# Second layer of a top-1 mixture: 128 tokens in one form and 448 in the other, with a new order of work

## The chip, the cores and the metric

The kernel runs on one core of a Trainium2 chip. The metric is the device time of one execution in microseconds, lower is better. The engines are named as in the profile: PE is TensorE, with PEld for its weight loads, DVE is VectorE, ACT is ScalarE, POOL is GpSimd, and SP is SyncE, which issues all DMAs here.

## The reference, cut to what matters

An attention over 32 memory slots feeds a mixture of 8 experts, of which each token uses one. The expert of a token is the argmax of its own gate or, where a local gate is 0.5 or more, that of the token before it.

```python
# q, k, v: (8, 8, 576, 64); phi: (8, 8, 576, 32); w1: (8, 512, 1024); w2: (8, 1024, 512)
a = softmax(phi, axis=2)                     # over the 576 tokens
k_m = einsum('bhsm,bhsd->bhmd', a, k); v_m = einsum('bhsm,bhsd->bhmd', a, v)
x = softmax(q @ k_m.T / 8) @ v_m             # heads side by side: (8, 576, 512)
for b in range(8):
    for s in range(576):
        e = fresh argmax of x[b, s] @ w_gate, or the expert of token s - 1
        p = softmax(x[b, s] @ w_gate)
        out[b, s] = p[e] * (relu(x[b, s] @ w1[e]) @ w2[e])
```

## The kernel before, in words

The kernel works batch by batch, 576 tokens each. For each batch it takes the expert of the first token and runs all 576 tokens through that expert; the probability of a token is set to zero where it has another expert. Pairs of batch and expert that remain are listed on the chip, and a loop at the end adds them.

For one batch, `hidden` computes the first layer: the matrix `G` (value memory times w1, from `w_pg` and `w_G`) against the attention weights `ah` and `al`. Values are held as two parts, high and low, in fp32r, and each product takes three matmuls: high by high, and both mixed terms. The result goes through the ReLU on ACT (L1109) and its low part through DVE (L1111) into `h`. Tokens are taken in `HALVES`, 256 and 320, so that `hidden` makes 4 groups of 12 matmuls of 256 columns and 8 groups of 6 of 320 columns.

The second layer has two forms. In the token form (`second`, L1139 to L1141) a block of 128 tokens stands as weights in the array and W2 streams past with 512 columns; the block takes 8 x 3 matmuls. In the turned form (`second_turned`, L1189 to L1191) a block of 128 output columns of W2 stands as weights and tokens stream past; there are 4 such blocks with 8 x 3 matmuls each, and each ends with a transpose on DVE (L1195) and a multiply by the probabilities on POOL (L1196). Batches 0 to 6 do tokens 0 to 255 in the token form (two blocks) and 256 to 575 in the turned form (320 columns). Batch 7 does everything in the token form: four blocks of 128, of which the last is done in two halves of 256 columns, and one block of 64 tokens, whose high and low parts stand side by side as 128 weights (L1163).

W2 is split by `w_split` on ACT and POOL, one of 8 pieces at a time; `t_evict` and `t_store` bring out a block of the token form, `o_store` the turned part with four DMAs.

The order of all work is written out by hand. `SCHEDULE` is a text with one line for each `yield` of `hidden`, `second` and `second_turned`; the steps of a line are issued to the engines' queues right after that group of matmuls. Steps are named with their batch, as `2 choice` or `2 pg 0`, and look ahead: most of the attention of batch b + 1 is issued among the matmuls of batch b. Each engine works through its queue in order. `BANKS` says for the small matmul steps which of the three PSUM pools their tile is taken from: "a" (3 banks), "h" (3 banks, first layer) or "o" (2 banks, `po` of the second layer).

Steps that are named below: `pg 0` and `pg 1` multiply the value memory by w1 (L1068, needs w1 loaded); `choice` finds the first token's expert on DVE (L871 to L873); `expert` lets SP read it, upon which SP issues `w1 0` (L1034); `a psc` makes scores on PE, `a turn` transposes them (L786); `g cols` makes columns of probabilities (L1001 on DVE, L1007 to L1017 on ACT); `g present` is a reduction on DVE (L992, L993); `z qT 0` is a transpose on DVE (L741); `warm b` and `warm u` are matmuls on zeros.

Of the kernel before, what the change touches and what calls it, by code (L numbers as in the profile page):

```python
# [48 lines left out]
0 split 1, 1 z qT 0, 0 split 2
0 split 3, 1 pT  # L50
1 q 1
1 a qT 0, 0 g kept

0 g carry, 0 split 4, 1 a qT 1


0 split 5, 0 split 6, 1 z qT 1, 0 at store
2 phi, 0 g exp, 1 kvT, 1 a psc, 0 split 7, 1 pgg
1 a turn
0 g prob  # L60
1 a mx, 0 g cols, 1 a sub, 2 colmax
1 a exp, 2 q 0, 0 evict 0, 1 a sum, 1 a inv, 1 a mul
# [18 lines left out]
2 kvT
2 a psc

1 split 1, 2 a turn
1 split 2
1 split 3
1 split 4, 2 z psc, 2 z turn, 2 a mx, 3 q 0, 2 pgg
3 colmax, 2 ggt, 1 split 5, 2 z mx
1 split 6, 2 a sub, 0 store 0, 0 store
1 split 7, 2 z sub, 0 store 1  # L90
2 a exp, 3 z qT 0
3 pm, 3 mc

2 a sum
3 kv, 2 z exp, 2 z sum, 2 z inv, 2 a inv, 1 g cols

3 pm2, 2 a mul, 1 evict 0, 2 z mul, 1 g present, 3 cx
2 a at

1 evict 1, 2 z at, 3 sub 1, 3 a qT 0, 2 g pl, 2 pl0, 2 g lt, 2 a ah, 3 exp 1, 2 g L  # L100
3 sub 0, 2 choice, 2 g fresh, 2 g kept, 3 q 1, 3 z qT 1
# [15 lines left out]
2 split 4, 3 a sub  # L120
# [8 lines left out]
4 kv, 3 z sub, 3 expert, 3 w1 0, 4 asum, 3 z exp, 3 z sum
2 g cols, 3 z inv  # L130
3 z mul
3 z at, 2 g present, 4 a qT 0, 1 kv store, 4 q 1, 4 pkv 0, 3 w1 1, 4 pkv 1, 5 phi, 3 w2 0, 3 pg 0, 5 q 0, 4 sums, 3 g pl, 3 z ah
3 g lt, 2 evict 0, 4 rinv, 4 z qT 0, 3 g L

3 G 0, 4 kvn, 4 z qT 1, 3 z al, 4 a qT 1, 4 pT
4 kvT, 4 a psc, 2 evict 1, 3 g fresh, 4 a turn, 4 a mx, 3 pg 1, 4 pgg, 5 colmax, 4 a sub, 4 ggt, 3 g kept
3 a al, 2 kv store


4 a exp, 4 a sum, 3 at store, 3 G 1  # L140
# [3 lines left out]
4 a inv, 3 g carry, 3 w2 1, 5 a qT 0  # L144


5 pm, 4 a mul, 4 a at
5 mc, 3 split 0

4 pl0, 4 z psc, 4 z turn, 4 choice, 5 pm2, 5 kv, 5 cx, 5 sub 0  # L150
4 expert, 3 split 1
5 sub 1, 4 z mx, 3 split 2, 4 a ah, 4 kv store, 4 a al, 3 split 3

5 q 1

3 g exp
3 split 4, 3 split 5, 5 exp 0, 2 store 1, 4 z sub  # L160


4 w1 0, 4 w1 1, 5 exp 1

3 split 6, 5 asum, 4 pg 0, 4 z exp, 3 g prob, 4 z sum, 5 a qT 1, 4 z inv, 5 pkv 0, 6 phi, 3 split 7, 5 z qT 0, 3 g cols, 5 pkv 1, 5 sums, 3 g present, 4 z mul, 5 z qT 1
# [3 lines left out]
5 rinv, 5 kvn, 4 z at, 4 g pl, 4 pg 1  # L169
6 colmax, 6 pm, 3 evict 0, 5 pT, 4 g lt, 4 G 1, 4 g L, 4 w2 0, 6 mc, 4 z ah, 5 kvT  # L170
3 store 0, 4 g fresh


4 z al, 4 G 0
5 pgg, 5 a psc, 5 a turn, 5 z psc, 2 store, 5 a mx, 5 ggt, 6 pm2, 6 cx, 5 kv store, 5 z turn

5 a sub, 6 sub 1, 6 q 0, 6 exp 1, 5 z mx, 4 g kept
3 evict 1, 6 sub 0
# [5 lines left out]
4 split 0, 4 split 1, 4 split 2, 5 a exp, 5 z sub, 5 a sum, 5 a inv, 4 split 3, 4 w2 1, 4 split 4, 4 split 5  # L184

6 exp 0, 5 a mul, 6 kv, 4 at store

5 a at, 6 q 1
5 z exp
2 store 0, 4 split 6, 5 z sum  # L190

5 a ah, 5 z inv, 4 g exp, 5 pl0, 5 choice


5 z mul, 5 expert
5 z at
6 asum, 5 w1 0, 5 w1 1

6 a qT 0, 7 phi, 6 pkv 0, 5 pg 0, 6 pkv 1, 6 sums, 4 split 7, 6 z qT 0, 4 g carry, 5 G 0
# [8 lines left out]
6 a exp, 6 a sum, 5 g exp, 7 mc, 5 split 0, 4 g present  # L210
# [48 lines left out]

5 g present
6 split 7
6 g exp, 6 g kept
7 pl0, 7 z psc


5 store, 7 choice
7 z turn, 7 z mx, 7 kv store, 7 z sub, 7 a ah  # L270
7 z exp, 7 expert, 6 g carry, 7 z sum

7 w1 0

7 w1 1

7 z inv, 7 z mul
7 z at
7 z ah, 7 pg 0, 5 store 1, 7 pg 1, 7 a al, 6 g prob, 7 g pl, 6 g cols, 6 evict 0
6 evict 1  # L280

7 G 0, 7 g lt
7 g L, 7 w2 0, 7 g fresh, 7 at store
6 g present
# [1261 lines left out]
```

## Time and profile before

| | us |
|---|---|
| median of three runs (397.38 to 398.92) | 398.43 |
| the profiled execution | 401.71 |
| its span, first to last instruction | 399.9 |
| PE busy in it | 386.5 |
| DVE busy in it | 282.4 |

The span leaves out 1.8 us that lie around it. Busy time is a sum over the span; it does not say which engine a stage waits for. Matmuls overlap each other, so that the mean of one is a latency and not its cost.

### The profile page before, as it was taken

The numbers are of one execution on the slowest core, as the hardware profiler recorded it, in microseconds if no ns is written. First come the engines' busy times: TensorE is split into PE (matmuls) and PEld (weight loads), VectorE is DVE, ScalarE is ACT, GpSimd is POOL, SyncE is SP. The second block draws the span as 40 slices with busy tenths as digits, with TensorE's granted clock in tenths as the row PEclk, the third lists the DMA queues.
The fourth block names the chain that finished last, engine by engine and source line by source line (L and its number), as shares of the span: only waits on it lengthen the run. The fifth ranks groups of instructions, "written<-read, shape, count | busy, mean of one in ns | idle before, by whom it ended". The sixth has DMA issues, their size and how long they took to land.

```text
span 399.9 us, 10792 instructions
## 1 busy us (share of the span) xinstructions
PE 386.5 (97%) x4336; PEld 335.2 (84%) x4336; DVE 282.4 (71%) x702; ACT 176.7 (44%) x437; POOL 151.1 (38%) x162
## 2 busy tenths in 40 slices
PE   8689999999998999999999999999999999999996
PEld 4476988899887887889878998799888998799885
DVE  4477899988988589786797779757845678456330
ACT  2236644447352584326653552515633653435311
POOL 1006471525330963129504741309412651057000
PEclk9789999999999999999999999999999999999999
DMA  7959869988969787979787937998680028702011
GB/s 226 315 188 330 169 166 263 354 218 190 294 165 373 171 303 174 297 221 301 243 256 178 324 82 277 351 233 225 216 290 8 2 80 318 268 1 67 27 41 57
DMA packets 115918, 82.59 MB, mean 207 GB/s; under 512 B 70100, under 2 KB 89560, under 8 KB 115864
## 3 DMA queue, kind: packets, MB, share of 16 engines
q1 hardware_dynamic: 115864, 81.86, 69.4%
q8 instruction: 35, 0.57, 0.6%
q14 instruction: 19, 0.16, 0.1%
HBM read 66.60 MB, written 15.24 MB: 205 GB/s over the span
## 4 chain that ended last, share of the span: by engine, by line
PE 48%; SPq 5%; DMA 5%; DVE 3%; issue 1%; ACT 1%; DVEq 0%
PE ph L1101 15%; PE po L1139 5%; PE po L1140 5%; PE po L1141 5%; DMA att_d<-at 4%; SPq L493 4%; PE po L1189 4%; PE po L1191 4%; PE po L1190 4%; PE pg L1068 2%; PE pkv L648 2%; DMA q_t<-in_q_dram 1%; PE po L1163 1%; PE psc L773 1%; DVE qT L741 1%
## 5 line engine op out<-in xcount | busy, mean ns | idle before, releaser
L1056 POOL TENSOR_TENSOR w2l<-raw,w2h 128x512 fp32r<-128x512 f32 x64 | 83.3, 1326 | 58.7 <-ACT w2h L1055 35.2
L1101 PE MATMUL ph<-ah,Gh 128*128 128x256 f32 (+1 forms) x256 | 73.4, 301 | 0.5 <-DVE h L1111 0.4
L1101 PE MATMUL ph<-ah,Gl 128*128 128x256 f32 (+1 forms) x256 | 72.0, 295 | 0.0
L1189 PE MATMUL po<-h,w2l 128*128 128x320 f32 x224 | 71.1, 317 | 0.1
L1111 DVE SCALAR_TENSOR_TENSOR h<-ph,h 128x320 fp32r<-128x320 f32 (+2 forms) x104 | 52.3, 517 | 24.8 <-ACT h L1109 24.4
L1191 PE MATMUL po<-h,w2h 128*128 128x320 f32 x224 | 69.2, 309 | 0.0
L1190 PE MATMUL po<-h,w2h 128*128 128x320 f32 x224 | 69.2, 309 | 0.0
L1109 ACT ACTIVATE h<-ph 128x320 fp32r<-128x320 f32 (+1 forms) x96 | 46.8, 492 | 38.6 <-PE ph L1101 38.3
L1139 PE MATMUL po<-w2h,h 128*128 128x512 f32 (+1 forms) x152 | 58.9, 388 | 0.0
L1140 PE MATMUL po<-w2l,h 128*128 128x512 f32 (+1 forms) x152 | 57.6, 379 | 0.0
L1141 PE MATMUL po<-w2h,h 128*128 128x512 f32 (+1 forms) x152 | 57.5, 378 | 0.0
L1101 PE MATMUL ph<-al,Gh 128*128 128x256 f32 (+1 forms) x256 | 55.0, 296 | 0.0
L842 POOL TENSOR_TENSOR al<-at,ah 128x576 fp32r<-128x576 f32 (+1 forms) x18 | 23.1, 1288 | 73.7 <-ACT ah L838 73.7
L1101 PEld LDWEIGHTS ph<-ah,Gh 128*128 128x128 f32 x256 | 48.1, 188 | 2.6 <-DVE h L1111 0.9
L1196 POOL TENSOR_TENSOR oT<-oT,gT 128x320 f32<-128x320 f32 x28 | 21.9, 787 | 74.0 <-DVE oT L1195 41.3
L1055 ACT ACTIVATE w2h<-raw 128x512 fp32r<-128x512 f32 x64 | 38.0, 624 | 25.9 <-PE po L1191 19.4
L1101 PEld LDWEIGHTS ph<-ah,Gl 128*128 128x128 f32 x256 | 48.1, 188 | 0.2 <-DVE Gl L1083 0.2
L1189 PEld LDWEIGHTS po<-h,w2l 128*128 128x128 f32 x224 | 42.1, 188 | 2.2 <-issue 1.1
L1190 PEld LDWEIGHTS po<-h,w2h 128*128 128x128 f32 x224 | 42.1, 188 | 0.1
L1191 PEld LDWEIGHTS po<-h,w2h 128*128 128x128 f32 x224 | 42.0, 188 | 0.0
L1101 PEld LDWEIGHTS ph<-al,Gh 128*128 128x128 f32 x256 | 41.2, 189 | 0.1
L1139 PEld LDWEIGHTS po<-w2h,h 128*128 128x128 f32 x152 | 28.6, 188 | 6.5 <-issue 1.6
(162 smaller groups left out, 591.4 us busy)
## 6 DMA issues: line engine op xcount, KB each, us to landing
raw<-in_moe_w_dram SPq DMA_DIRECT2D x34, 512.0 KB, 6.9
raw<-in_moe_w_dram SPq DMA_DIRECT2D x15, 1024.0 KB, 7.0
kv_t<-in_k_dram SPq DMA_DIRECT2D x7, 1152.0 KB, 7.4
kv_t<-in_v_dram SPq DMA_DIRECT2D x7, 1152.0 KB, 9.8
q_t<-in_q_dram SPq DMA_DIRECT2D x112, 72.0 KB, 3.7
...
```

The source lines that it names most:

```text
L842: (eng or nc.gpsimd).tensor_tensor(out=st.al[:, gs, ss], in0=st.at[:, gs, ss], in1=st.ah[:, gs, ss], op=ALU.subtract)
L1055: nc.scalar.activation(h, src, AF.Copy)
L1056: nc.gpsimd.tensor_tensor(out=l, in0=src, in1=h, op=ALU.subtract)
L1101: nc.tensor.matmul(pv[:, c - c0], lhsT=lt[:, g, cs], rhs=rt[:, g, s0 : s0 + n], start=(i == 0), stop=(i == 5),)
L1109: nc.scalar.activation(hc[:, :, 0:n], pv, AF.Relu)
L1111: nc.vector.scalar_tensor_tensor(out=hc[:, :, o : o + z - a], in0=pv[:, :, a:z], scalar=0.0, in1=hc[:, :, a:z], op0=ALU.max, op1=ALU.subtract,
L1139: nc.tensor.matmul(po[:, c0:c1], lhsT=h[:, c, th], rhs=hi, start=(c == 0), stop=False)
L1140: nc.tensor.matmul(po[:, c0:c1], lhsT=h[:, c, th], rhs=lo, start=False, stop=False)
L1141: nc.tensor.matmul(po[:, c0:c1], lhsT=h[:, c, tl], rhs=hi, start=False, stop=(c == FC - 1))
L1189: nc.tensor.matmul(po[:, 0:n], lhsT=lo, rhs=h[:, c, 0:n], start=(c == 0), stop=False)
L1190: nc.tensor.matmul(po[:, 0:n], lhsT=hi, rhs=h[:, c, 0:n], start=False, stop=False)
L1191: nc.tensor.matmul(po[:, 0:n], lhsT=hi, rhs=h[:, c, n : 2 * n], start=False, stop=(c == FC - 1))
```

## The change

The second layer takes tokens 0 to 127 in the token form and 128 to 575, 448 tokens, in the turned form, in all batches. In batch 7 the turned form comes first, and the token block follows in two halves of 256 output columns. The tile `h` is one tile for all tokens and no longer two; `oT` grows from 10 to 14 blocks of 32 tokens; the tile `q0e` takes a buffer of `ot`. Batches have 32 lines of the order and batch 7 has 36, where they had 36 and 34. From the end of the first line on (behind `0 G hi`) the order is new, and so is `BANKS`.

```diff
 BANKS = {
-    "a psc": {1: "h", 3: "h", 4: "h", 5: "h", 7: "h"},
+    'a psc': {1: 'h', 3: 'o', 5: 'h', 7: 'o', 2: 'o', 0: 'o'},
...
+    'pkv': {1: 'o', 0: 'h'},
...
 SCHEDULE = """
...
-0 z sub, 1 exp 0, 1 warm u, 0 warm b, 1 exp 1, 0 pg 1, 0 G 1, 1 asum, 0 w2 0, 0 z exp, 0 z sum, 1 q 0, 0 warm b
-0 w2 1, 0 z inv, 0 split 0, 0 z mul, 0 z at
+1 exp 1, 0 pg 1, 0 G 1, 1 asum, 0 w2 0, 0 z exp, 0 z sum, 1 q 0, 0 z inv, 0 z mul, 0 split 0, 0 split 1
+0 z at, 1 pkv 0, 0 w2 1
...
-2 g exp, 2 w1 0
-2 w1 1, 3 asum, 3 pkv 0, 3 pkv 1, 2 pg 0, 2 g carry, 3 sums, 0 kv store, 3 rinv
+1 g present, 2 expert
+2 g fresh, 0 kv store, 3 exp 0
+2 g exp, 3 pkv 0, 2 a al
+3 asum, 3 pkv 1, 2 w1 0, 2 pg 0, 2 g kept, 3 sums, 2 g carry, 4 phi, 3 rinv, 2 w2 0, 3 kvn, 2 g prob
...
     HALVES = ((0, 256), (256, 320))
+    TURN = 128
...
-    q0e = const.tile([64, HG, NG, D], F32, name="q0e")
+    q0t = pf.tile([P, DM], F32, tag="ot", name="q0e", bufs=2)
+    q0e = q0t[0:64].rearrange("p (h g d) -> p h g d", h=HG, g=NG)
...
     def hidden(G, ah, al, res, turned=False):
 
+        h = pf.tile([P, FC, 2 * S], F32R, tag="h", name="h", bufs=1)
+        res.append(h)
         for s0, n in HALVES:
 
-            ht = pf.tile([P, FC, 2 * n], F32R, tag=f"h{s0}", name=f"h{s0}", bufs=1)
-            res.append(ht)
...
+                if end:
+                    nc.scalar.activation(by_chunk(ot)[:, :, j0 : j0 + 2], pv, AF.Copy, scale=gt()[:, t : t + 1])
+                    cs = slice(128 * j0, 128 * j0 + 256)
+                    nc.sync.dma_start(out=out[B - 1, t * P : t * P + P, cs], in_=ot[:, cs])
...
-        s0, n = HALVES[1]
-        h = ht[1]
+        n, h = S - TURN, ht[0]
         st.oT = oT = pf.tile([P, n // 32, 4, 32], F32, tag="oT", name="oT", bufs=1)
         for dc in range(4):
             po = ps_o.tile([P, DM], F32, tag="po", name="po")
             for c in range(FC):
                 hi, lo = (w[:, P * dc : P * dc + P] for w in W2[c])
-                nc.tensor.matmul(po[:, 0:n], lhsT=lo, rhs=h[:, c, 0:n], start=(c == 0), stop=False)
+                nc.tensor.matmul(po[:, 0:n], lhsT=lo, rhs=h[:, c, TURN:S], start=(c == 0), stop=False)
...
     def moe(st):
-        b = st.b
-        ht = []
-        turned = b < B - 1
-        yield from hidden(st.G, st.ah, st.al, ht, turned)
+        ht, last = [], st.b == B - 1
+        yield from hidden(st.G, st.ah, st.al, ht, True)
         st.ot = {}
...
+        if last:
+            yield from second_turned(ht, st.W2, st)
+        for t in range(TURN // P):
+            st.ot[t] = []
+            yield from second(ht, st.W2, t, lambda: st.g[0], st.ot[t], last, True)
+        if not last:
             yield from second_turned(ht, st.W2, st)
```

## Rows read from the trace of the kernel before

**Rows 1.** The page's totals: busy us, share of the span, instructions.

```profile
span 399.9 us, 10792 instructions
...
PE 386.5 (97%) x4336; PEld 335.2 (84%) x4336; DVE 282.4 (71%) x702; ACT 176.7 (44%) x437; POOL 151.1 (38%) x162
```

**Rows 2.** Stages: length, then busy us of PE, PEld, DVE, ACT, POOL; clock.

```profile
33.20:83.00 49.80, 49.35 (x717) 41.76 (x710) 44.10 (x100) 26.25 (x65) 24.10 (x22) 1.00 0.89 239
...
83.00:131.00 48.00, 46.10 (x502) 41.56 (x501) 41.03 (x109) 22.24 (x58) 16.23 (x14) 1.00 0.92 255
...
265.00:311.00 46.00, 46.00 (x513) 41.35 (x512) 29.37 (x69) 20.76 (x47) 20.26 (x18) 1.00 0.63 197
```

**Rows 3.** Waits of PE from 131 us on: total, times, longest.

```profile
PE pl L858 <- DVE at L834: 0.6, 2, 0.3
...
PE ph L1101 <- DVE h L1111: 0.4, 1, 0.4
```

**Rows 4.** Timeline, choice to pg 0: start, length, [idle before <-releaser].

```profile
75.01 0.66 PE L1068 MATMUL pg<-raw,kvT 64*32 64x512 f32 x8 [0.37 <-DMA raw<-in_moe_w_dram]
...
113.91 0.14 DVE L873 TENSOR_SCALAR c<-ei 1x1 f32<-1x1 uint32 x1
...
114.45 0.40 SPq L1034 DMA_DIRECT2D raw<-in_moe_w_dram  x1
...
121.82 0.66 PE L1068 MATMUL pg<-raw,kvT 64*32 64x512 f32 x8 [1.90 <-DMA raw<-in_moe_w_dram]
```

**Rows 5.** Chain of work that ended last: start, us, count.

```profile
357.65 12.80 PE ph L1101 x96
...
381.35 3.63 PE po L1163 x16
```

**Rows 6.** PE by line and shape: busy us, mean ns of one.

```profile
L1189 PE MATMUL po<-h,w2l 128*128 128x320 f32 x224 | 71.1, 317 | 0.1
...
L1139 PE MATMUL po<-w2h,h 128*128 128x512 f32 x136 | 54.4, 400 | 0.0
```

**Rows 7.** Timeline of PE where big matmuls follow small ones.

```profile
57.28 0.25 PE L714 MATMUL pgg<-wg,kvT 64*32 64x9 f32 x16
...
57.46 0.50 PE L1139 MATMUL po<-w2h,h 128*128 128x512 f32 x1
...
57.80 0.40 PE L1140 MATMUL po<-w2l,h 128*128 128x512 f32 x1
```

**Rows 8.** DVE and POOL by line and shape: busy us, mean ns of one.

```profile
L741 DVE STREAM_TRANSPOSE qT<-q_t 128x576 f32<-128x576 f32 x28 | 21.1, 757 | 1.8 <-issue 1.0 <-DMA att_d<-at 0.7
...
L1195 DVE STREAM_TRANSPOSE oT<-po 128x320 f32<-128x320 f32 x28 | 14.1, 502 | 19.9 <-PE po L1191 18.9 <-issue 1.0
...
L553 DVE TENSOR_REDUCE cm<-phi_t 128x128 f32<-128x1152 f32 x6 | 13.6, 2260 | 1.1 <-DMA phi_t<-in_phi_dram 1.1
...
L786 DVE STREAM_TRANSPOSE sc<-psc 128x288 f32<-128x288 f32 x30 | 12.6, 457 | 5.9 <-PE psc L773 5.4 <-PE pl L858 0.5
...
L992 DVE TENSOR_REDUCE pres<-oh 32x8 f32<-32x144 f32 x8 | 3.2, 400 | 0.0
...
L993 DVE SCALAR_TENSOR_TENSOR pres<-code,rb,pres 32x8 f32<-32x8 f32 x8 | 2.8, 348 | 0.3
...
L893 DVE STREAM_TRANSPOSE lt<-pl 128x128 f32<-128x128 f32 x8 | 2.4, 302 | 0.8 <-PE pl L858 0.4 <-PE pl L883 0.4
...
L1196 POOL TENSOR_TENSOR oT<-oT,gT 128x320 f32<-128x320 f32 x28 | 21.9, 787 | 74.0 <-DVE oT L1195 41.3 <-ACT Gh L1081 28.3 <-DMA q_t<-in_q_dram 2.9
```

**Rows 9.** Timeline of ACT, last batch.

```profile
371.95 0.87 ACT L1010 ACTIVATE gt<-gs 32x5 f32<-32x5 f32 x4 [3.04 <-DVE gs L1001]
...
373.28 0.44 ACT L1109 ACTIVATE h<-ph 128x320 fp32r<-128x320 f32 x1
```

**Rows 10.** Timeline of the tail.

```profile
395.89 0.28 PE L1141 MATMUL po<-w2h,h 128*128 128x256 f32 x1
...
396.21 0.47 ACT L1149 ACTIVATE ot<-po,gt 128x256 f32<-128x256 f32 x1 [2.40 <-PE po L1141]
```

More of the change, by code (lines that the diff above doesn't have):

```diff
@@ L48 @@
+1 exp 1, 0 pg 1, 0 G 1, 1 asum, 0 w2 0, 0 z exp, 0 z sum, 1 q 0, 0 z inv, 0 z mul, 0 split 0, 0 split 1
+0 z at, 1 pkv 0, 0 w2 1
+0 z ah, 0 g pl, 0 z al, 0 g lt, 1 pkv 1, 0 g L, 1 sums, 1 rinv, 0 g fresh
 1 kvn
[L49 to L62, printed above, removed]
@@ L81 @@
[L81 to L101, printed above, removed]
@@ L129 @@
[L129 to L144, printed above, removed]
@@ L147 @@
[L147 to L170, printed above, removed]
@@ L171 @@
[L171 to L201, printed above, removed]
@@ L254 @@
-6 split 1, 7 a inv, 7 a mul, 5 store 0, 6 split 2, 6 g fresh, 6 split 3, 7 ggt
-7 z qT 1, 6 split 4, 6 split 5
+0 split 2, 1 z qT 0
+0 split 3
+1 a qT 0
+1 q 1, 0 g kept
+0 g carry, 1 pT, 0 split 4
+1 a qT 1, 1 kvT, 0 split 5
+2 phi, 1 pgg, 1 z qT 1, 0 split 6, 0 split 7, 1 a psc
+0 g exp, 1 z psc, 2 kv, 1 a turn
+1 ggt, 0 g prob, 0 g cols, 1 a mx, 1 a sub, 2 colmax, 0 at store, 1 a exp, 1 a sum, 1 a inv, 1 a mul
+1 a at, 1 pl0, 0 evict 0, 1 a ah, 1 z turn, 1 choice, 2 pm, 1 a al
+1 z mx, 2 mc, 2 q 0, 1 expert, 1 z sub, 1 z exp
@@ new lines @@
+2 pm2, 1 z sum, 1 z inv, 2 a qT 0
+1 w1 0, 2 cx, 2 sub 1
+2 z qT 0
+2 sub 0, 0 g present, 1 z mul
+1 pg 0, 1 w1 1, 2 q 1, 1 z at, 2 exp 0
+1 G 0, 1 g pl, 3 phi, 2 pkv 0, 1 g lt, 2 exp 1, 2 pkv 1, 1 g L, 1 z ah, 2 asum, 1 z al, 1 g fresh, 1 pg 1, 1 G 1, 2 z qT 1, 1 g exp, 2 sums, 1 w2 0, 2 rinv
+2 kvn, 1 g kept, 1 g carry
+1 w2 1
+2 a qT 1
+2 pT, 2 kvT, 1 split 0, 1 g prob
+3 q 0, 1 split 1, 1 split 2, 2 z psc, 2 a psc
+2 a turn
+1 split 3, 1 kv store
+1 split 4, 2 pgg, 2 z turn, 2 a mx
+2 ggt, 1 split 5, 1 at store, 2 a sub, 3 colmax, 1 split 6
@@ new lines @@
+2 split 2, 3 a qT 1, 3 pT
+4 colmax, 3 kvT, 2 z ah, 2 w2 1
+2 z al, 4 pm, 4 q 0, 3 pgg, 4 mc, 2 split 3, 2 pg 1, 3 a psc, 2 split 4, 3 ggt, 3 a turn, 2 G 1, 4 pm2
+3 a mx, 1 store, 2 split 5, 3 a sub
+4 cx
+3 a exp, 3 a sum
+3 a inv, 2 at store
+4 z qT 0, 4 sub 0, 4 sub 1
+4 exp 0, 3 a mul
+3 a at
+4 kv
+3 pl0, 3 choice, 3 z psc, 2 split 6, 3 expert, 3 z turn, 3 z mx, 4 exp 1, 2 split 7, 3 z sub
+3 w1 0, 4 a qT 0, 3 z exp, 3 z sum, 3 a ah, 4 asum, 3 z inv
+3 z mul, 3 z at, 4 pkv 0, 4 q 1, 3 w1 1, 3 pg 0, 4 pkv 1, 2 g cols, 4 sums, 3 g pl
@@ new lines @@
+3 g lt, 4 rinv, 2 kv store, 2 evict 0, 4 a qT 1, 3 z ah, 5 phi, 3 z al, 3 g L, 3 a al, 3 G 0, 4 z qT 1
+4 kvn, 2 g present, 4 pT
+4 kvT, 3 g fresh, 4 a psc, 4 a turn, 4 a mx, 4 a sub, 3 w2 0
+5 colmax
+4 pgg, 3 pg 1, 4 a exp, 3 G 1, 3 at store, 3 split 0, 5 q 0, 3 g kept, 4 a sum
+4 ggt, 5 pm
+4 a inv, 4 a mul, 5 q 1, 4 a at, 5 mc, 3 g exp
+5 kv, 3 split 1, 3 g carry
+4 z psc, 4 a ah, 4 z turn, 4 pl0, 5 a qT 0, 3 w2 1, 5 pm2, 2 store, 5 cx
+5 sub 0
+4 z mx, 3 split 2, 5 sub 1
+3 split 3, 4 choice, 4 expert
@@ new lines @@
+5 a exp, 6 sub 1, 5 z turn
+4 split 0
+6 q 0, 6 q 1, 5 z mx
+4 split 1, 5 a sum
+4 split 2, 5 a inv, 6 exp 1, 5 z sub, 6 sub 0
+4 split 3, 6 kv, 5 a mul
+4 split 4, 5 a at, 5 z exp, 5 z sum
+5 pl0
+5 choice
+5 a ah
+4 split 5
+3 store
+6 exp 0, 5 z inv
+5 expert
+5 z mul, 5 w1 0, 6 z qT 1, 6 asum, 4 split 6, 5 z at
+5 w1 1, 5 pg 0, 7 phi, 4 g carry, 6 pkv 0, 4 kv store, 6 pkv 1, 6 sums, 4 split 7
+5 z ah
+6 rinv, 6 kvn, 5 G 0, 6 a qT 0
+6 pT, 6 kvT
+4 g prob, 4 g cols, 6 a qT 1, 5 w2 0, 6 pgg, 6 ggt, 0 pairs, 5 pg 1, 5 z al, 7 colmax, 6 a psc, 5 g pl, 5 kv store, 5 g lt, 4 evict 0, 6 z qT 0, 5 a al
@@ new lines @@
+6 a turn, 4 g present, 6 a mx, 7 pm, 5 g L, 3 store 0, 7 mc, 5 g fresh, 5 G 1
+5 at store, 6 a sub, 6 a exp, 4 store 0, 5 w2 1, 6 a sum, 5 split 0
+7 q 0, 5 split 1, 6 a inv, 5 g kept
+7 pm2, 7 kv, 7 cx, 6 a mul, 5 split 2
+6 a at, 5 split 3
+6 z psc, 6 pl0, 5 g exp, 5 split 4, 6 z turn
+7 sub 0
+6 z mx, 5 split 5
+6 choice, 4 store
+6 z sub
+7 sub 1, 7 z qT 0, 7 a qT 0, 3 kv store, 7 exp 0, 7 exp 1, 6 expert, 6 w1 0, 6 w1 1, 6 z exp
+7 asum, 6 z sum
+7 pkv 0, 5 split 6, 6 a ah, 6 w2 0, 5 g carry, 7 q 1, 7 pkv 1, 5 split 7, 5 g prob, 6 w2 1, 7 sums, 7 rinv, 6 pg 0, 7 kvn
@@ L257 @@
+6 kv store, 5 g present
+6 z inv, 6 z mul, 5 g cols, 7 pT, 5 evict 0
+6 z at
+7 a qT 1, 6 z ah
+6 a al
+7 kvT
+6 g pl, 6 G 0, 7 a psc, 7 a turn, 7 z qT 1, 6 pg 1, 7 kv store, 6 z al, 7 pgg
+6 g lt
+7 a mx, 7 a sub, 6 g L
+7 a exp, 7 ggt, 7 a sum, 6 g fresh
+6 split 0, 6 split 1, 6 split 2, 7 a inv, 6 at store
+7 a mul, 6 G 1, 6 split 3
+6 split 4
 7 a at
+7 z psc, 7 pl0
+6 split 5
 6 split 6
[L263 to L284, printed above, removed]
-7 g kept
-6 store 0
-7 g carry, 7 G 1, 7 split 0, 7 split 1, 7 z al
-7 w2 1
-7 g exp
-7 split 2, 7 split 3, 7 split 4, 6 store 1
-7 split 5
-7 split 6, 4 store 1
-7 split 7, 7 g prob, 7 g cols, 6 store
+7 z turn
+7 z mx, 6 split 7, 7 choice, 5 store, 7 z sub, 7 z exp
@@ L305 @@
+7 expert, 6 g kept, 7 z sum, 6 g exp
+6 g carry, 5 store 0
+6 g prob, 7 w1 0, 7 z inv
+7 a ah, 7 z mul, 6 g cols, 7 z at, 7 w1 1
+7 z ah
+7 g pl, 7 a al, 6 g present, 7 pg 0, 7 pg 1, 7 G 0
+6 evict 0, 7 w2 0, 7 w2 1, 7 g lt
+7 g L, 7 z al
+7 g fresh
+7 g kept
+7 split 0
+7 G 1
+7 split 1
+7 split 2
+7 g carry
+7 split 3
+7 split 4
+7 split 5, 7 split 6
+7 g exp, 7 at store
+7 split 7
+7 g prob
+6 store 0, 7 g cols
+6 store
 7 g present
 7 list
+7 store
 """
```

166 lines of the change are left out of this document (56 added, 110 removed), and 28 rows, old and new, of the table BANKS.

## The prediction

> **What bounds the kernel now.** I read the page's totals first, then the stages, then the waits of TensorE, then one stretch of timeline. [rows 1]: PE is busy for 386.5 of 399.9 us, DVE for 282.4. That is an average, so [rows 2] gives the stages: from 33.2 to 83 us PE works 49.35 of 49.80 us and DVE 44.10 of the same 49.80, and up to 131 us DVE still has 41.03 of 48.00. The granted clock is 1.00 of full speed, 2.4 GHz, in both. After 131 us PE waits for another engine three times only, 1.0 us in all [rows 3]. So past the first two batches the time is the sum of what PE does, and only work taken from PE can shorten it.
>
> Ahead of that the order matters. [rows 4] shows batch 2's gate: DVE finishes the choice of the expert (L873) at 114.05 us, SP issues the load of that expert's w1 at 114.45, and PE starts `pg 0` (L1068) at 121.82 after 1.90 us of idling for that load. Batch 1 shows the same at 75.01, with 0.37 us. The choice stands in DVE's queue behind all that DVE was given before, and DVE is nearly full there, so `pg 0` of batch 2 is a fence: what PE saves ahead of it mostly turns into a longer wait at it.
>
> **What a matmul costs.** The durations by line and shape are latencies of overlapping instructions and must not be multiplied. The price is the distance between starts. The chain [rows 5] has one clean stretch of 96 first-layer matmuls, 48 of 256 and 48 of 320 columns, in 12.80 us. Their 27,648 columns at 2.4 GHz are 11.52 us, which leaves 1.28 / 96 = 13.3 ns for each instruction. Sixteen matmuls of 512 columns took 3.63 us: 3.41 for columns, 13.5 ns each left. So three widths give one line, columns / 2.4 GHz + 13.3 ns: 120.0, 146.7 and 226.7 ns, and 200.0 ns for the new width of 448.
>
> **The change part by part.** *The split, batches 0 to 6.* Columns stay the same; the number of matmuls falls. Before, a batch has 48 of 512 (token form, L1139 to L1141) and 96 of 320 (turned form, L1189 to L1191), as the counts 136 and 224 of one line of each in [rows 6] confirm (7 x 16 + 24, 7 x 32): 10.88 + 14.08 = 24.96 us. After, 24 of 512 and 96 of 448: 5.44 + 19.20 = 24.64 us. That is 0.32 us a batch and 2.24 in seven.
>
> *Batch 7.* Before: 72 and 16 of 512 and 48 of 256, 16.32 + 3.63 + 5.76 = 25.71 us. After: 96 of 448 and 48 of 256, 19.20 + 5.76 = 24.96. That is 0.75 us less, because the 64-token block that was done with half of its columns spent twice disappears. PE's saving is 2.99 us in all. The final 48 now read W2 in runs of 64 columns; no row has that read on such a matmul. Bounds: nothing, or a second pass over the 5.12 us of columns; all their neighbours keep the line above, so I take nothing.
>
> *The order.* A return from a block of small matmuls on part of the array costs extra: in [rows 7] the first big matmul after one starts 0.34 us ahead of the next instead of 0.227, about 0.11 us. Counted in the two orders (lines behind the first with such a step), there are 12 returns up to `pg 0` of batch 2 and 21 after it; the new order has 15 and 22. So +0.3 us ahead of the fence and +0.1 us behind it. Two `warm b` (one matmul of 512 columns in bf16 each) go: at 2.4 GHz their columns are 0.43 us of PE, ahead of the fence.
>
> *DVE and the fence.* From [rows 8]: a transpose of 320 columns out of PSUM takes 502 ns, one of 128 takes 302, so 448 takes 502 + 128 x 1.04 = 635 ns, an estimate from these two rows. Up to batch 2's choice, the new order gives DVE four transposes that are 0.133 us longer and one block more (0.64), +1.17 us; it puts behind the choice a `g present` (0.40 + 0.35) and a `z qT 0` (0.76), -1.51 us. Net -0.34: the choice comes about 0.3 us earlier and no more, as DVE has no other slack. PE's own path to that `pg 0` is shorter by 66.72 - 66.48 = 0.24 us of big matmuls (batch 0 with 24.96 against 24.64, batch 1 with 16.16 against 16.24 of second layer up to there, first layer the same, so -0.32 + 0.08) and 0.43 of warm-up, less 0.3 of returns. PE is therefore about 0.4 us early at a door that opens 0.3 us early. Gain at the fence: 0.3 us. Bounds: none, if any new wait holds DVE; 1.9 + 0.3 us, if the load lands so early that the whole wait goes.
>
> *Behind the fence* 2.99 - 0.24 = 2.75 us of matmul time are still to be saved, less 0.1 of returns.
>
> *Moved and hidden work.* POOL's multiply grows from 787 ns [rows 8] to about 1.1 us, four a batch; POOL has 24.10 of 49.80 us in the fullest stretch [rows 2], so it hides. One eviction on ACT goes, and one `ot` store; SP issues the same four `oT` stores, longer by 40%, and nobody waits for one except the next batch's `oT` a batch later. The tile `h` of the first layer's results is now one buffer: the next batch's first write waits for the last matmul of this one, which PE has passed anyway, at no cost. `q0e` shares a buffer with `ot`, first written tens of us later.
>
> *Batch 7 now starts with the turned form,* which reads the second half of `h` at once. In [rows 9] ACT stood 3.04 us before the gate columns, so the last evictions of `h` began at 373.28, 2.83 us after PE had left the first layer (357.65 + 12.80, [rows 5]). The token form had cover of 10.9 us for it; the turned form reaches the last chunk after 7 x 0.6 = 4.2 us. Moving the step two groups earlier than the end leaves 0 to 0.5 us of wait; I take 0.2.
>
> *The tail* is the same: the last eviction of 256 columns began 0.32 us after the last matmul's start [rows 10], followed by one store. The four `oT` stores of batch 7 are issued some 5 us ahead. Nothing is added; at most the last store shares the queues, 0.5 us.
>
> *Waits of the new order.* Nearly every step stands elsewhere. The old order loses 1.0 us behind the fence [rows 3], low for 270 us. Bounds for the new one are 0 and, at the rate of the front (2.3 us in two batches), some 5 us. I take 1.5, near the old row, since DVE is freer there (29.37 of 46.00 us from 265 us on, [rows 2]): +0.5.
>
> **Sum.** -0.3 - 2.75 + 0.1 + 0.2 + 0.5 = -2.25 us. Against the profiled execution: span 399.9 to 397.65, and with the 1.8 us around it 401.7 to 399.5. That execution is 3.3 us above the median of the runs, 398.43; the saving is in fixed work and carries over: 398.43 - 2.25 = 396.2 us.
>
> **Rivals.** *The fixed 13.3 ns is not saved.* If it belonged to the stream of columns and not to the instruction, only the 2,048 columns less of batch 7 would count, 0.85 us; with 0.1 + 0.2 + 0.5 against it and nothing at the fence the time is 398.4. Against it speaks that 256, 320 and 512 columns leave the same remainder; chance 0.04. The Trainium skill ("TensorE: Matmul & The Clock Gate", section "Back-to-back issue gap") gives an isolated gap of N / 2.4 + 2.5 ns; by that figure the 168 matmuls less of batches 0 to 6 would save 0.42 us and not 2.24. The trace's 13.3 ns differs from it, and the measurement decides.
>
> *The waits eat the gain.* For it speaks that DVE has 0.53 us more per batch and the gate, the weights and the scores all come through it. Waits of 0.3 to 4.2 us beyond my count give 396.5 to 400.4: chance 0.31.
>
> *Slower: two banks too few.* The new table of places puts the score tiles `a psc` of batches 2, 3 and 7 into the two `po` banks of the second layer, where before only single tiles stood. The next block on PE then waits until DVE has turned both, 2 x 0.457 us, behind whatever is queued, at worst a reduction of 2.26 us [rows 8]: about 2.3 us each when bare. One such place is swallowed by the gain; from two on, 4.6 us, the change loses: 398.43 - 2.25 + 4.6 = 400.8. Against it: most of these steps stand in or beside the first layer, which needs other banks. Chance 0.13.
>
> *A freer fence.* The new order asks for batch 2's k and v earlier; if w1 of batches 1 and 2 lands sooner, another 1 to 2 us go: 394 or below, chance 0.05.
>
> **How the numbers follow.** My own case, with no more than small misses (393.5 to 396.4), has 0.47. A difference within 0.5%, 2 us, is about what a measurement of this kernel can't tell from none. Faster by more needs under 396.4: 0.47 + 0.05 = 0.52. Within: 0.31 + 0.04 = 0.35. Slower: 0.13. The range for 8 in 10 goes from 393.2, where the fence frees or the new order waits less, to 400.0, which takes in most of the eaten gain.
>
> **What would show it.** Starts of the 448-column matmuls 0.200 us apart, and 4.8 us for an undisturbed block of 24; `pg 0` of batch 2 still waiting for its load near 121.5 us; PE's other waits after it near 1.5 us; the last batch's turned form beginning with less than 0.5 us of idling. I am wrong if the 448s are further apart, if PE idles before turned blocks for DVE's transposes or `a turn`, or if `pg 0` of batch 2 moves by more than a microsecond.

## The result, and the profile after

| | before | after |
|---|---|---|
| median of 22 runs each, us | 397.62 | 400.36 |
| ratio of the runs, 95% interval | | 1.0069 (1.005 to 1.0088) |
| profiled execution, us | 401.71 | 401.16 |
| first layer of batch 0 starts (profile) | 33.23 | 30.65 |
| PE ends (profile) | 396.17 | 393.04 |
| from there to the end of the span | 3.74 | 6.18 |

The change makes the kernel slower by 2.7 us, where 2.25 us less were forecast. The two profiled executions can't be laid side by side as they are: the one of before, on which the prediction rests, ran its front at a lower clock. This is the stretch from 10 to 30 us in it, in a second trace of the same kernel (label k1_before, below) and in the changed kernel; the columns are those of [rows 2].

```profile
10.00:30.00 20.00, 15.53 (x335) 11.50 (x334) 11.27 (x39) 5.98 (x18) 0.00 (x0) 0.83 0.83 251
```

```profile
10.00:30.00 20.00, 14.91 (x377) 10.51 (x377) 12.03 (x42) 7.16 (x22) 0.80 (x1) 1.00 0.90 284
```

```profile
10.00:30.00 20.00, 15.38 (x406) 10.89 (x409) 13.30 (x44) 6.92 (x22) 1.94 (x3) 1.00 0.95 301
```

At the full clock before has its first layer of batch 0 at 31.35 us, PE's end at 393.62 and the end of the span 3.85 us behind that. From that first layer on, PE takes 362.27 us before and 362.39 after: nothing is saved on PE. And 2.3 us are lost behind it. These two facts are the case.

The page's totals and the stages after, which answer [rows 1] and [rows 2]; a row of 131 to 175 us is added:

```profile
span 399.2 us, 10444 instructions
...
PE 384.7 (96%) x4169; PEld 329.5 (83%) x4174; DVE 289.6 (73%) x697; ACT 171.2 (43%) x428; POOL 161.5 (40%) x166
```

```profile
33.20:83.00 49.80, 49.44 (x664) 41.70 (x657) 44.92 (x110) 24.67 (x63) 23.69 (x21) 1.00 0.88 224
83.00:131.00 48.00, 48.00 (x520) 40.32 (x519) 40.67 (x98) 24.16 (x62) 24.10 (x20) 1.00 0.88 257
131.00:175.00 44.00, 42.27 (x458) 35.68 (x457) 36.50 (x77) 18.77 (x47) 15.76 (x13) 1.00 0.87 234
265.00:311.00 46.00, 46.00 (x485) 40.74 (x484) 29.87 (x69) 20.55 (x51) 20.47 (x18) 1.00 0.64 186
```

PE is still busy nearly all the time, with 167 matmuls less by the page. The stall that stood ahead of 131 us is gone (48.00 of 48.00, against 46.10), and 1.7 us of idling stand in the next stage instead. Behind the first layer of batch 0 PE waits three times, which answers [rows 3]. The first row is that stall, the only wait behind 131 us; the two of 0.2 us lie ahead of it:

```profile
PE pg L1045 <- DMA raw<-in_moe_w_dram: 1.6, 1, 1.6
PE pl L835 <- DVE at L811: 0.2, 1, 0.2
PE ph L1083 <- POOL al L819: 0.2, 1, 0.2
```

**The new width.** Timeline of PE in the last batch: the first matmul of 448 columns, and the first of the 256-column ones behind its 96. No stall lies between them.

```profile
367.67 0.37 PE L1168 MATMUL po<-h,w2l 128*128 128x448 f32 x1
...
387.13 0.28 PE L1121 MATMUL po<-w2h,h 128*128 128x256 f32 x1
```

That is 19.46 us for 96, 202.7 ns each, and not 200.0. The first layer of the same batch, in the chain of work that ended last, is what it was in [rows 5]:

```profile
355.02 12.81 PE ph L1083 x96
```
The latency by line, the answer to [rows 6], doesn't tell the price; DVE's 637 ns and POOL's 956, which answer [rows 8], stand against estimates of 635 and 1,100:

```profile
L1168 PE MATMUL po<-h,w2l 128*128 128x448 f32 x256 | 96.0, 375 | 0.0
```

```profile
L1174 DVE STREAM_TRANSPOSE oT<-po 128x448 f32<-128x448 f32 x32 | 20.4, 637 | 23.5 <-PE po L1170 22.0 <-issue 1.4
```

```profile
L1175 POOL TENSOR_TENSOR oT<-oT,gT 128x448 f32<-128x448 f32 x32 | 30.6, 956 | 121.1 <-DVE oT L1174 63.9 <-issue 16.1 <-DMA raw<-in_moe_w_dram 15.6
```

**The end.** The last issues of SP and the last eviction on ACT (start, length), which answer [rows 10]: two blocks from the second trace of before, then two from after.

```profile
391.28 3.21 SPq L1151 DMA_DIRECT2D out_dram<-ot  x2
```

```profile
393.66 0.47 ACT L1149 ACTIVATE ot<-po,gt 128x256 f32<-128x256 f32 x1 [2.40 <-PE po L1141]
```

```profile
389.03 3.22 SPq L1180 DMA_DIRECT2D out_dram<-oT  x4
392.35 1.80 SPq L1129 DMA_DIRECT2D out_dram<-ot  x2
```

```profile
393.08 0.47 ACT L1127 ACTIVATE ot<-po,gt 128x256 f32<-128x256 f32 x1 [2.35 <-PE po L1123]
```

ACT is done 0.51 us behind PE in both. What differs stands in the waits of SP's own queue from 380 us on (total, times, longest; L1527 before and L1501 after are the conditional loop over listed pairs, which nothing enters here), and in the DMA issues of the last microseconds (count, size, time to landing), before and then after:

```profile
SPq L1527 <- SPq L1527: 1.0, 2, 0.5
```

```profile
SPq L1501 <- SPq L1501: 3.0, 1, 3.0
```

```profile
out_dram<-ot SPq DMA_DIRECT2D x2, 128.0 KB, 1.8
```

```profile
out_dram<-oT SPq DMA_DIRECT2D x4, 224.0 KB, 3.2
out_dram<-ot SPq DMA_DIRECT2D x2, 128.0 KB, 3.7
```

SP branches past the loop, and its next instruction comes 2.98 us later, where it took 0.46 before. The last stores also land later. Which of the two counts is the question of half of the experiments.

### The profile page after: what moved, and what is told of

It is laid out like the page before. It is cut to its first block, busy times and chain, and to the rows that moved or that the text cites. A ratio compares the mean times of both kernels' runs of the same rounds, so it can differ in the third digit from the quotient of the medians.

```text
span 399.2 us, 10444 instructions
## 1 busy us (share of the span) xinstructions
PE 384.7 (96%) x4169; PEld 329.5 (83%) x4174; DVE 289.6 (73%) x697; ACT 171.2 (43%) x428; POOL 161.5 (40%) x166
## 4 chain that ended last, share of the span: by engine, by line
PE 86%; DMA 4%; DVE 3%; POOL 2%; ACT 1%; SPq 1%; issue 1%; DVEq 0%; POOLq 0%
PE ph L1083 25%; PE po L1168 13%; PE po L1169 12%; PE po L1170 12%; PE pg L1045 4%; PE po L1121 3%; PE pkv L625 3%; PE po L1123 3%; PE po L1122 3%; PE psc L750 2%; DMA kv_t<-in_k_dram 2%; DMA raw<-in_moe_w_dram 2%; PE pl L860 1%; PE wp L525 1%; PE pq L737 1%
## 5 line engine op out<-in xcount | busy, mean ns | idle before, releaser
L1033 POOL TENSOR_TENSOR w2l<-raw,w2h 128x512 fp32r<-128x512 f32 x64 | 84.5, 1341 | 61.9 <-ACT w2h L1032 50.1
L1168 PE MATMUL po<-h,w2l 128*128 128x448 f32 x256 | 96.0, 375 | 0.0
L1169 PE MATMUL po<-h,w2h 128*128 128x448 f32 x256 | 93.5, 365 | 0.0
L1170 PE MATMUL po<-h,w2h 128*128 128x448 f32 x256 | 93.5, 365 | 0.0
L1175 POOL TENSOR_TENSOR oT<-oT,gT 128x448 f32<-128x448 f32 x32 | 30.6, 956 | 121.1 <-DVE oT L1174 63.9
L1093 DVE SCALAR_TENSOR_TENSOR h<-ph,h 128x320 fp32r<-128x320 f32 (+1 forms) x96 | 51.9, 549 | 27.2 <-ACT h L1091 26.6
L1168 PEld LDWEIGHTS po<-h,w2l 128*128 128x128 f32 x256 | 48.1, 188 | 9.0 <-issue 4.0
L1170 PEld LDWEIGHTS po<-h,w2h 128*128 128x128 f32 x256 | 48.1, 188 | 3.9
L1169 PEld LDWEIGHTS po<-h,w2h 128*128 128x128 f32 x256 | 48.2, 188 | 3.6
L1174 DVE STREAM_TRANSPOSE oT<-po 128x448 f32<-128x448 f32 x32 | 20.4, 637 | 23.5 <-PE po L1170 22.0
L1060 DVE TENSOR_TENSOR Gl<-pg,Gh 128x512 fp32r<-128x512 f32 (+1 forms) x34 | 20.6, 649 | 9.4 <-ACT Gh L1058 9.3
L1121 PE MATMUL po<-w2h,h 128*128 128x512 f32 (+1 forms) x72 | 27.1, 376 | 0.0
L1123 PE MATMUL po<-w2h,h 128*128 128x512 f32 (+1 forms) x72 | 26.4, 367 | 0.0
```

The source lines that it names most:

```text
L1033: nc.gpsimd.tensor_tensor(out=l, in0=src, in1=h, op=ALU.subtract)
L1093: nc.vector.scalar_tensor_tensor(out=hc[:, :, o : o + z - a], in0=pv[:, :, a:z], scalar=0.0, in1=hc[:, :, s0 + a : s0 + z], op0=ALU.max, o ...
L1121: nc.tensor.matmul(pv, lhsT=h[:, c, th], rhs=hi, start=(c == 0), stop=False)
L1123: nc.tensor.matmul(pv, lhsT=h[:, c, tl], rhs=hi, start=False, stop=(c == FC - 1))
L1168: nc.tensor.matmul(po[:, 0:n], lhsT=lo, rhs=h[:, c, TURN:S], start=(c == 0), stop=False)
L1169: nc.tensor.matmul(po[:, 0:n], lhsT=hi, rhs=h[:, c, TURN:S], start=False, stop=False)
```

## The experiments

The first four were made when only the late end and the missing gain of PE were known. My theory was that the last two stores stand behind the four of the turned part.

**k1_before.** No edit.

> The kernel before once more, unchanged, for a second trace. In the first one the granted clock was 0.80 and 0.86 from 10 to 30 us; in the trace of the changed kernel it was 1.00 there and the first layer of batch 0 began 2.58 us earlier. If that is the clock alone, this trace has its first layer of batch 0 near 30.7 us, the end of PE near 393.6 and the span near 397.3. If the later start belongs to the kernel, PE ends near 396.2 again.

First layer at 31.35, PE's end 393.62, span 397.5. So the late start went with the clock; what is left against 30.65 is no more than the traces at full clock differ by (30.17 in k8_short, with the old order, to 31.06 in k10_both, with the new one). One stall of its front is another one (1.46 us at 118.95 where the first trace had 1.90 at `pg 0`); everything behind 131 us repeats.

**k2_nostore and k3_last.** The first takes one step out of the order; the second gives batch 7 its old loop:

```diff
-7 store
+
```

```diff
...
-        if last:
-            yield from second_turned(ht, st.W2, st)
-        for t in range(TURN // P):
...
+        for t in range(TURN // P) if turned else (0, 1, 4, 2, 3):
...
```

> The changed kernel, with the four stores of the last batch's turned tokens left out (that part of the output is not written). Theory, the tail: the last two stores of the token block queue behind these 0.9 MB, which costs 2.4 us behind the end of PE (6.2 us against 3.7 before). Then PE ends as in the changed kernel, the rest behind it is 3.7 us, and the time is 400.4 - 2.4 = 398.0, a ratio of 1.001 to before. Rival, all is lost on PE's side: the stores are hidden, 400.4 and 1.007.

> The changed kernel with the last batch alone put back: five token blocks, each stored as it is done, the last in two halves. PE has 0.75 us more matmul time. By the tail theory 400.4 + 0.75 - 2.4 = 398.7, ratio 1.003, and 3.7 us behind the end of PE. By the rival (the tail costs nothing, the loss is in batches 0 to 6): 401.1, ratio 1.009.

The ratios to before are 1.005 (1.0021 to 1.008) and 1.0036 (1.0011 to 1.006). The rest behind PE is 5.47 and 5.40 us, hardly less than 6.18. So the theory fell as it was put: with the stores away SP still waits 2.5 us behind its branch.

```profile
SPq L1501 <- SPq L1501: 2.5, 1, 2.5
```

```profile
SPq L1499 <- SPq L1499: 2.5, 1, 2.5
```

The second number of use is batch 7 itself. From the first matmul of its second layer to PE's end it is 25.87 us in the second trace of before and 25.37 after: 0.50 us saved, where 0.75 was forecast.

**k4_order.** The old order with the new split in batches 0 to 6.

> The order of the kernel before and its table of places, with the new split in batches 0 to 6 alone: its 36 lines a batch are laid on 32 by the time of the matmuls; the last batch is as before. Theory, the new order eats the gain of the split: here 2.24 us of matmul time are saved and the old waits stay, 397.6 - 1.7 to 2.2 = 395.4 to 395.9, ratio 0.994 to 0.996. Rival, the fences (loads of w1, DVE) take what the split saves whatever the order: 397.0 to 398, ratio 0.998 to 1.001.

418.42 us, ratio 1.0495: outside both. PE idles in nearly every stage: 3.4 us between the first layers of batches 1 and 2 (most at `pg 0`, 123.1 us) and 4.3 between those of 4 and 5 (most at a `pm` behind DVE's reduction, 271.2 us); the granted clock is 0.94 in both of these stretches. An order laid on fewer lines by time alone loses 20 us, so the run says nothing on the split; it says that the split can't be had without a new order.

**k6_pad, k5_hint and k8_short** are about the branch. The first cuts late stores into pieces, so that SP has 18 more instructions; the second gives SP a prefetch hint (its edit is below); the third takes ten stores out of the kernel before.

```diff
-        tc.mark_branch_hint_location("rare", None, [mybir.EngineType.PE])
+        tc.mark_branch_hint_location("rare", None, [mybir.EngineType.PE, mybir.EngineType.SP])
```

> The changed kernel with 18 more DMA issues on SP and nothing else: stores of batches 5 and 6, late in the kernel, are cut into smaller pieces. Theory, the branch: at the end SP skips the loop over listed pairs; in the changed kernel its first instruction behind the skip came 2.98 us after the branch (2.49 and 2.45 in the two kernels made from it), in the kernel before 0.45 both times, and the branch is SP's 450th instruction or so there and the 466th here. With 18 more in front of it the branch stands behind that of the kernel before, and the gap is 0.45 us: the time falls by 2.0 to 2.5 us, to a ratio of about 1.001. Rival, the gap follows from the stores at the end: nothing changes, ratio 1.005 to 1.007.

> The changed kernel, in which SP too gets the prefetch hint for that branch that PE has already. By the branch theory the gap of 2.5 to 3 us falls to 0.5 us and the time by 2.0 to 2.5 us, if a hint at the head of SP's stream, some 450 instructions ahead, still holds there; if it doesn't, nothing changes. By the rival (stores) nothing changes either.

> The kernel before without ten of its stores (the second token block of batches 0 to 6, the first of 4 to 6: that part of the output is not written). It does less. By the branch theory its branch now stands some 14 places earlier in SP's stream, where that of the changed kernel stands, so the gap behind it grows from 0.45 to 2.5 us and the kernel becomes 2 us slower: ratio 1.004 to 1.006. Rival: 1.000 or less, since nothing but stores has gone.

Measured: k6_pad 1.010 (1.0048 to 1.0153), gap 2.18 us, a miss. k5_hint 1.0033 (1.0005 to 1.006), gap 0.46: the hint closes it, yet the rest behind PE only falls from 6.18 to 5.32. k8_short 1.0075 (1.0041 to 1.0108), gap 2.45: the kernel before gets the gap of the changed kernel when 14 instructions ahead of its branch are taken out. (Its time says more than that: PE took 2.9 us longer too, spread over several waits, which I can't explain.)

k5_hint shows why neither cure was enough. Its waits of SP, and its last stores:

```profile
SPq L1501 <- SPq L1501: 2.5, 4, 1.6
```

```profile
out_dram<-ot SPq DMA_DIRECT2D x2, 128.0 KB, 3.9
```

SP is past the branch at once, and then waits 1.65 us for the last stores to land. So code and stores run side by side, and each alone may hold the end.

**k10_both, k9_last_hint and k11_256** test that. k10 joins k2 and k5, k9 joins k3 and k5; k11 gives batch 7 alone another split:

```diff
...
-        n, h = S - TURN, ht[0]
+        T, h = turn(st.b), ht[0]
+        n = S - T
...
+    def turn(b):
+        return TURN if b < B - 1 else 2 * TURN
...
```

> The changed kernel without the last batch's four stores of turned tokens (that part of the output is not written) and with the prefetch hint on SP. So far, from the end of PE to the end of the span: 6.18 us as it is, 5.47 without the stores, 5.32 with the hint, 3.74 and 3.85 in the kernel before. Theory, two things side by side, each of which would be enough: SP's code behind the branch comes late (2.5 us), and the last two stores land late behind 0.9 MB (3.9 us from issue against 1.8). With both taken away the rest is 3.8 to 3.9 us and the time falls by 2.3 us against the changed kernel: ratio to before 0.998 to 1.001. Rival, one of the two is only noise and a third thing holds the end: 5.3 us again, ratio 1.003.

> The kernel with the last batch put back (whole output; it had 5.40 us behind PE's end, a gap of 2.45 us behind the branch, and 1.0036) with the hint on SP as well. By the theory of two causes the stores of its last batch are out of the way, so that the hint alone takes the rest to 3.8 us: 1.6 us less, ratio 1.000 or a little under. Rival: 5.3 us again, ratio 1.0036.

> The changed kernel with the hint on SP, and in the last batch alone 256 tokens in the token form and 320 in the turned form, the turned form first: its four stores go out one block of 5.4 us earlier. By the distances that were measured (448 columns 202.6 ns, 320 columns 146.7, 512 columns 226.7) PE's work is 14.08 + 5.44 + 5.76 = 25.28 us there against 25.21, so nothing is lost on PE; the rest behind PE is 3.8 us. Against the run with the hint alone (ratio 1.0033) that is 1.4 us less: 0.999 to 1.000. Rival, the price of 448 columns is not what holds PE and a split with more blocks loses 0.3 us and more.

| us behind PE's end | four stores at the end | out of the way |
|---|---|---|
| code late | 6.18 (after) | 5.47 (k2), 5.40 (k3), 5.39 (k8) |
| code there (hint) | 5.32 (k5) | 4.02 (k10), 4.58 (k9), 3.61 (k11) |

The kernel before has 3.74 and 3.85. So the theory of two causes holds in k10 and k11. k9 keeps some 0.7 us more: its last store takes 2.6 us to land, against 1.7 in k11, and SP waits 1.2 us for it. Why it is slower there was not tested. SP's wait in k10 and the landing of its last stores:

```profile
SPq L1501 <- SPq L1501: 1.1, 2, 0.6
```

```profile
out_dram<-ot SPq DMA_DIRECT2D x2, 128.0 KB, 1.7
```

The ratios are 1.0021 (0.999 to 1.0052) for k10, 1.0047 (1.0011 to 1.0083) for k9 and 1.0035 (1.0007 to 1.0063) for k11. With the end repaired the changed kernel is about level with before, and not ahead of it: k10, which leaves out a part of the output, can't be told from it, and the other two are still a little slower, where 1.000 or less was expected. In k11 PE also waits 0.46 us at 370.3 for ACT's last part of `h`: a turned block of 320 columns gets to the last chunk sooner than one of 448. From the first matmul of its second layer batch 7 takes 26.33 us there, against 25.38 in k5, where 0.07 more was expected; so the rival, a loss on PE, came true in part, by that wait. No version with the whole output beats the kernel before.

**k7_width and k12_width** measure the price of a matmul by its width, one width in each batch:

```diff
...
+        a, w0 = ((0, 448), (64, 448), (128, 384), (128, 416), (64, 512), (96, 480), (128, 352), (128, 448))[st.b]
...
-                nc.tensor.matmul(po[:, 0:n], lhsT=lo, rhs=h[:, c, TURN:S], start=(c == 0), stop=False)
...
+                nc.tensor.matmul(po[:, 0:w0], lhsT=lo, rhs=h[:, c, a : a + w0], start=(c == 0), stop=False)
...
```

> The changed kernel, but the turned form streams another stretch of tokens in each batch (start and width: 0 and 448, 64 and 448, 128 and 384, 128 and 416, 64 and 512, 96 and 480, 128 and 352, 128 and 448), so that its output is not the reference's: for the distance between starts. In the changed kernel 448 columns took 202.7 ns and not 200.0. Theory, a matter of where the stretch begins: the starts at 0 and 64 give 200.0, the other widths lie on columns / 2.4 GHz + 13.3 ns (384: 173.3, 416: 186.7, 512: 226.7, 480: 213.3, 352: 160.0). Rival, a matter of the width itself or of the layout of the whole tile: 448 takes 202.7 from any start, and 416 or 480 may be off the line too.

> As the run with one width a batch, with others: 432, 464, 496, 504, 288, 400, 440 and 472 columns, all from token 64 (the output is not the reference's). On the line columns / 2.4 GHz + 13.3 ns they are 193.3, 206.7, 220.0, 223.3, 133.3, 180.0, 196.7 and 210.0. Measured so far against it: 352, 384, 416 and 512 on the line within 0.4, 448 at 202.6 (+2.6), 480 at 219.9 (+6.6). Theory, something that grows between 416 and 512 and is gone at 512: 432 within 1 ns of the line, 464 at +4 to +5, 496 and 504 above +7 unless they fall back like 512. Rival, only multiples of 32 are off: 440 and 504 on the line.

Mean distance between starts in ns, without the longest tenth of each batch (returns and waits); the line is columns / 2.4 GHz + 13.3:

| columns | line | measured | | columns | line | measured |
|---|---|---|---|---|---|---|
| 288 | 133.3 | 131.3 | | 448 | 200.0 | 202.3 to 203.7 |
| 352 | 160.0 | 159.9 | | 464 | 206.7 | 209.0 |
| 384 | 173.3 | 173.5 | | 472 | 210.0 | 213.1 |
| 400 | 180.0 | 179.9 | | 480 | 213.3 | 219.9 |
| 416 | 186.7 | 186.9 | | 496 | 220.0 | 222.6 |
| 432 | 193.3 | 195.1 | | 504 | 223.3 | 226.7 |
| 440 | 196.7 | 199.7 | | 512 | 226.7 | 227.1 |

One undisturbed block of 24 at 480 columns, its first matmul and the next block's (5.28 us, 220.0 each):

```profile
306.47 0.38 PE L1169 MATMUL po<-h,w2l 128*128 128x480 f32 x1
...
311.75 0.28 PE L1083 MATMUL ph<-ah,Gh 128*128 128x256 f32 x1
```

Where the stretch begins doesn't matter: 448 costs 202.7, 203.7 and 202.3 from tokens 0, 64 and 128, and the batches of the changed kernel, all from 128, differ as much (202.2 to 203.6). Between 416 and 512 columns every width is above the line, by 1.8 to 6.6 ns. Both rules that I had for it missed (it isn't only multiples of 32, and it doesn't grow steadily), so the cause stays open; the price doesn't.

**k13_pad43 and k14_fence** settle two leftovers: the miss of k6_pad, and what holds PE behind the fence. k13 is k6 with more stores cut; k14 is k5 without the step `1 store`.

> The changed kernel with 43 more DMA issues on SP (stores of batches 2 to 6 in smaller pieces), after 18 more did not close the gap behind the branch (2.18 us). There the 8 KB of code came 0.64 us behind the branch (394.61 against 393.97), in the kernel before 1.96 us ahead of it (392.60 against 394.56). Theory, place and time: SP fetches the next piece when its stream comes to a fixed place, near instruction 465; with 18 more the branch stands just behind that place and SP gets there only 0.6 us ahead. With 43 more it passes the place some 25 instructions ahead, long before: the gap is 0.45 us, and the rest behind PE is then that of the stores alone, 5.3 us. Rival, place has nothing to do with it: a gap of 2.2 to 3 us again.

> The changed kernel with the hint on SP and without batch 1's four stores of turned tokens, 0.9 MB, which stand some 10 us ahead of the load of batch 3's w1 (that part of the output is not written). PE waits for that load or for the work around it at 152 to 154 us in every trace of the new order, 0.8 to 1.8 us. Theory, the queues of the DMA are full there: without the stores the wait falls below 0.3 us and PE comes from the first layer of batch 0 to that of batch 3 in 145.6 us (146.5 to 148.2 so far). Rival, it is the choice of the expert that comes late: the wait stays.

k13: gap 0.46 us, 5.26 us behind PE. So 18 more instructions were too few and 43 are enough, as the theory of place and time has it; the theory itself is inferred. The DMA of code around the branch fits it: after, in the 3 us behind its branch, then in the second trace of before, in the 2.6 us ahead of it (queue, count, MB, share of time):

```profile
q14 instruction: 1, 0.01, 1.2%
```

```profile
q8 instruction: 1, 0.02, 2.2%
q14 instruction: 1, 0.01, 1.2%
```

Before gets a piece of code on this queue ahead of the branch and none in the 0.46 us behind it; after gets it behind. (That this piece is SP's is inferred from its time: the queue serves other engines too.) The Trainium skill ("Runtime: NRT & Kernel Launch", section "Instruction fetch mechanics") says that code is fetched ahead in sequence only and that a taken branch to a piece not yet there waits for a DMA. The traces agree as far as they show it, with 2.18 to 2.98 us here.

k14: PE waits 1.65 us at 153.10 in the changed kernel, 0.98 us in k5, and not at all here. Timelines of DVE's choice, SP's issue of w1 and `pg 0` for batch 3 after, which answer [rows 4], and then PE's 140 to 155 us in the changed kernel and in k14:

```profile
144.45 0.14 DVE L850 TENSOR_SCALAR c<-ei 1x1 f32<-1x1 uint32 x1
```

```profile
144.98 0.38 SPq L1011 DMA_DIRECT2D raw<-in_moe_w_dram  x1
```

```profile
153.10 0.66 PE L1045 MATMUL pg<-raw,kvT 64*32 64x512 f32 x8 [1.65 <-DMA raw<-in_moe_w_dram]
```

```profile
140.00:155.00 15.00, 13.28 (x214) 10.13 (x220) 12.16 (x24) 6.87 (x19) 2.52 (x2) 1.00 0.88 262
```

```profile
140.00:155.00 15.00, 15.00 (x266) 12.07 (x264) 13.13 (x27) 6.47 (x16) 2.52 (x2) 1.00 0.72 200
```

The choice is in time; the load takes 8 us while the DMA has a busy share of 0.88, and without the 0.9 MB, at 0.72, the wait is gone. From the first layer of batch 0 to that of batch 3 PE takes 146.00 us in k14, where 145.6 was expected, 146.54 in k5, 146.5 to 148.2 in the traces of the new order with these stores and 147.3 in the second trace of before.

## Why the prediction was wrong

**The price of 448 columns** is the first step that failed: "So three widths give one line". The three widths lay on it, the fourth doesn't. A row at 202.6 ns makes 96 x 202.6 = 19.45 us of turned form, and a batch 24.89 us against 24.96. The saving is 0.07 us a batch and not 0.32, and 0.50 in batch 7 and not 0.75: 1.0 us in all and not 2.99. The mechanism was right (fewer matmuls, the same columns), its term was mis-sized by 2.0 us. I had named this as a sign of error ("if the 448s are further apart") and gave it no chance of its own; the rival that came near it, the fixed part not saved, had 0.04 for another reason. The isolated gap of the Trainium skill ("TensorE: Matmul & The Clock Gate", section "Back-to-back issue gap"), N / 2.4 + 2.5 ns, would be 189.2 ns at 448 columns; the runs lie above it at every width.

**The tail** is the second: "Nothing is added; at most the last store shares the queues, 0.5 us". It cost 2.3 us. Two things were missed. The sentence "nobody waits for one except the next batch's `oT`" holds for seven batches; in the last, the end of the kernel waits for all stores, and 0.9 MB were issued from 389.0 to 392.3 us, right ahead of the last store at 393.6. And the order of the last instructions on SP was not looked at: the change takes 16 instructions away ahead of a branch, which no row of work shows and the chain of work that ended last doesn't name.

**The order** is the third: "So +0.3 us ahead of the fence and +0.1 us behind it" for returns from small matmuls. All small matmuls together became 3.1 us dearer. Counted in the traces from each start to the next, without idle time and from batch 0's first layer on, they take 47.0 us in the second trace of before and 50.2 after, and 49.8 to 50.2 in the other five traces of the new order with the same work on PE. Busy time of the three largest groups by line and shape from 31 us on shows it too, before and then after:

```profile
L648 PE MATMUL pkv<-kv_t,phi_t 64*32 64x128 f32 x1008 | 16.6, 271 | 1.5 <-issue 1.5
L1068 PE MATMUL pg<-raw,kvT 64*32 64x512 f32 x240 | 16.3, 594 | 0.4 <-DMA raw<-in_moe_w_dram 0.4
L773 PE MATMUL psc<-qT,kvT 64*32 64x288 f32 x224 | 9.8, 412 | 0.0
```

```profile
L625 PE MATMUL pkv<-kv_t,phi_t 64*32 64x128 f32 x1008 | 17.2, 272 | 0.1
L1045 PE MATMUL pg<-raw,kvT 64*32 64x512 f32 x240 | 17.1, 595 | 1.6 <-DMA raw<-in_moe_w_dram 1.6
L750 PE MATMUL psc<-qT,kvT 64*32 64x288 f32 x224 | 10.3, 411 | 0.1
```

Their number is the same; where they stand is not. The 16 matmuls of a `pg` hold PE for 1.02 us where they stand alone between big ones (71.65 us after) and for 0.86 beside other small steps (from 74.08). How much of the 3.1 us comes from that, and how much from the new table of places, was not tested.

**The fence** came earlier than forecast: `pg 0` of batch 2 at 116.51 without a wait, against 119.20 in the second trace of before and 121.82 in [rows 4]. From batch 0's first layer that is 2.0 us sooner than in the second trace, so the rival of a freer fence came true there. At batch 3's first layer nothing is left of it (147.47 us from that of batch 0, against 147.26); 1.65 us of it went at batch 3's fence, in the wait that k14 takes away. "The waits eat the gain" had 0.31 and is not what happened: behind batch 0's first layer PE idles 2.15 us after and 2.96 in the second trace of before. The wait from 131 us on, 1.65 us, is near the 1.5 that were taken.

**What was right:** the clock (1.00 in every stage read from 33 us on), DVE's price and that POOL's work hides, the free read of W2 in runs of 64 columns (starts 0.12 us apart from 387.13 on), the single `h`. Batch 7's wait for `h`, taken as 0.2 us, was none: ACT was done with it at 371.1 us, 3.5 us into the turned form (the answer to [rows 9]), and the last chunk is needed after 7 x 0.6 = 4.2.

```profile
370.35 0.77 ACT L1091 ACTIVATE h<-ph 128x320 fp32r<-128x320 f32 x2
```

And the two `po` banks, the slower rival, cost PE no wait in the trace.

**The sum again.** From batch 0's first layer to the end of the span the two traces at full clock differ by +2.45 us: second layer -1.26 (1.0 by the rows of widths), warm-up -1.03 (0.69 of it, `1 warm u`, only stands ahead of the first layer now), idle time -0.81, first layer +0.09, small matmuls +3.13, the rest behind PE's end +2.33. The runs differ by +2.7, with an interval of 2.0 to 3.5. This is one pair of traces: PE's time from batch 0's first layer to its end was 361.4 to 363.1 us in the six traces of the new order with the same work on PE, mostly by their idle time.
